# A late test of denominators, mean squares and decay with a branch to a float32 path, in a fused forgetting-attention and SwiGLU kernel

## The chip, the core and the metric

The kernel runs on one core of one Trainium2 chip. The metric is the device time of one launch in microseconds, the median of several runs; lower is better. The core has five engines with queues of their own: TensorE (PE, with its weight loads shown apart as PEld), VectorE (DVE), ScalarE (ACT), GpSimd (POOL) and SyncE (SP, which here only issues transfers). An engine takes its instructions in order; engines wait for one another on semaphores.

## What is computed

Attention with a forget gate, then a feed-forward block. B = 8, H = 8, S = 576, D = 64; the FFN has 4608 tokens, a width of 512 and 1536 hidden units.

```python
scores = scale * q @ k.T                       # per (b, h)
cum    = cumsum(log(clip(f, 1e-4, 1)))
scores = where(causal, -1e9, scores + cum[:, None] - cum[None, :])
attn   = exp(scores - max(scores)) ;  attn /= sum(attn) + 1e-9
x      = (attn @ v)  ->  (4608, 512)
xn     = x / sqrt(mean(x*x) + 1e-6) * rms_g
out    = (silu(xn @ w_gate) * (xn @ w_val)) @ w_out
```

## The kernel before

Attention goes by (batch, query block): four blocks of 128 rows per sequence and a last one of 64, the last ones of two batches joined in one tile. No row maximum is taken. Instead exp(mid - cum) for each key, `decT`, is multiplied into V (L528), with a column of the same factors beside it, so that the product of the exponentials with this V (L627) gives numerators and the denominator in one PSUM bank. DVE takes the reciprocal of the denominators (`rden`, L643) and multiplies (L645). The normal rows then are squared and summed (`ms`, L659 or L673), raised to -1/2 on POOL (L678), normalised (L689), transposed (on SP, L709) and go to the FFN in nine groups of 512 tokens: eight of the 128-row blocks, tile `xT`, and the ninth of all the 64-row blocks, tile `xTr`.

In the FFN a gate step (`gate`, L763) is: four matmuls with `wg` into one of four PSUM banks `ff` (L773), four with `wv` into another, tanh on ACT (`th`, L786), (th + 1) times the gate on DVE (`ga`, L788, after which the first bank is free), and ga times the value on DVE (`hT`, L780, after which the second bank is free). The projection (L807) takes twelve matmuls per 128 tokens, a copy out of PSUM (L821, on ACT; on DVE for the very last tile) and a transfer to the output (L829; L838 for the ninth group).

The order of all instructions is settled before anything runs: every step is a unit with an engine, an estimated duration, a key and dependencies, and `Plan.run` (L152) walks through time and gives each engine the ready unit with the lowest key; it also hands out the buffers of the rings, the four `ff` banks among them. `SHIFTS`, a table with one entry per unit, moves each key. The steps that the change touches: `emit_cum` (L367) builds `cum`, `mid`; `emit_const` (L342) fills constants on POOL; `rden` was two small tiles used in turn; the units run at L865, and after them the program ends, each engine going straight on to the closing block (L897), where SP waits for all transfers and the engines meet twice.

## Time and profile before

| | us |
|---|---|
| timed runs | 371.33, 372.7, 373.48 (median 372.7) |
| span of the profiled execution, first to last instruction | 370.3 |
| PE busy in the span | 354.5 (96%) |
| DVE, ACT, POOL busy | 231.8, 206.6, 188.4 |
| granted TensorE clock, mean | 1.000 |

The median of the timed runs is 2.4 us above the span of the profiled execution; its own time outside the span isn't recorded. In the timeline a row gives the start, the time to the end of the last of the instructions it joins, the engine, the line, output and input, how many instructions, and in brackets the idle time before them with what ended it. An engine's name with q (SPq, PEldq) is an instruction that its sequencer handles: a transfer's issue, a wait, a drain.

### The profile page before, as it was taken

What the parts mean: (1) busy time and instruction counts of PE and PEld (TensorE: products, weight loads), DVE (VectorE), ACT (ScalarE), POOL (GpSimd) and SP (SyncE); (2) the same over time, 40 slices, a digit from 0 to 9 for tenths busy, and PEclk for the clock granted to TensorE, in tenths of its full rate; (3) what the DMA queues carried; (4) which work ended last, traced back from release to release, by engine and by line L of the source; (5) the groups of instructions that cost most, each with busy time, mean ns of one, the idle gap of its engine ahead of it and who ended that gap; (6) DMA issues with size and microseconds to landing.
All of it is one profiled execution on the core that took longest, in us unless ns stands there. A gap on an engine that the chain in (4) does not pass through costs nothing.

```text
span 370.3 us, 9645 instructions
## 1 busy us (share of the span) xinstructions
PE 354.5 (96%) x3916; PEld 207.0 (56%) x3916; DVE 231.8 (63%) x457; ACT 206.6 (56%) x312; POOL 188.4 (51%) x253
## 2 busy tenths in 40 slices
PE   3878999999999999999999999999999999999995
PEld 1568977887754555554555454446544554444443
DVE  6666676677657786568764677455576436877210
ACT  5752676666766777756737776168835434233121
POOL 8954799979898737554995179524201110000000
PEclk9999999999999999999999999999999999999999
DMA  9999999999999992999999979963400121000124
GB/s 119 194 206 213 196 225 128 164 204 127 151 140 153 192 143 60 143 199 114 138 165 200 157 71 115 178 125 86 114 30 0 50 81 58 2 0 2 57 57 113
DMA packets 155965, 45.08 MB, mean 122 GB/s; under 512 B 145489, under 2 KB 150353, under 8 KB 155921
## 3 DMA queue, kind: packets, MB, share of 16 engines
q0 software_dynamic: 80896, 17.83, 57.0%
q1 hardware_dynamic: 74864, 26.51, 38.0%
q8 instruction: 30, 0.49, 0.6%
q14 instruction: 15, 0.11, 0.1%
q10 hardware_dynamic: 160, 0.13, 0.1%
HBM read 38.16 MB, written 9.44 MB: 129 GB/s over the span
## 4 chain that ended last, share of the span: by engine, by line
PE 88%; DMA 5%; POOL 3%; issue 1%; DVE 1%; ACT 0%; POOLq 0%; DVEq 0%; ACTq 0%
PE ff L773 49%; PE ff L807 24%; PE sc L557 7%; PE ff L627 7%; DMA qk<-in_q_dram 5%; POOL qk L401 1%; PE ff L507 1%; PE sc L568 1%; POOL PT L607 1%; POOL Vs L528 0%; PE ff L698 0%; ACT PT L599 0%; POOL rs L678 0%; PE ff L380 0%; ACT junk L659 0%
## 5 line engine op out<-in xcount | busy, mean ns | idle before, releaser
L599 ACT ACTIVATE PT<-sc 128x1024 bf16<-128x1024 f32 x100 | 98.2, 1022 | 33.3 <-PE sc L557 28.7
L788 DVE SCALAR_TENSOR_TENSOR ga<-th,ff 128x512 f32<-128x512 f32 x108 | 73.6, 686 | 50.1 <-ACT th L786 47.8
L807 PE MATMUL ff<-wo,hT 128*128 128x512 bf16 (+2 forms) x444 | 103.9, 373 | 0.0
L786 ACT ACTIVATE th<-ff 128x512 f32<-128x512 f32 x108 | 63.8, 597 | 61.8 <-PE ff L773 54.0
L773 PE MATMUL ff<-xT,wv 128*128 128x128 bf16 (+1 forms) x672 | 94.8, 288 | 0.1
L773 PE MATMUL ff<-xT,wg 128*128 128x128 bf16 (+1 forms) x672 | 93.9, 288 | 0.8 <-DVE xT L705 0.8
L780 DVE SCALAR_TENSOR_TENSOR hT<-ga,ff 128x512 bf16<-128x512 f32 x108 | 72.0, 684 | 24.3 <-PE ff L773 22.0
L773 PEld LDWEIGHTS <-wg 128*128 128x128 bf16 x720 | 54.1, 98 | 39.7 <-issue 0.9
L773 PEld LDWEIGHTS <-wv 128*128 128x128 bf16 x720 | 53.7, 98 | 37.7 <-DMA wv<-in_moe_w_val_dram 0.3
L607 POOL TENSOR_SCALAR_AFFINE_SELECT PT<-PT 128x1024 bf16<-128x1024 bf16 x32 | 36.8, 1154 | 54.1 <-ACT PT L599 54.1
L807 PEld LDWEIGHTS <-hT 128*128 128x128 bf16 x444 | 39.5, 98 | 40.0
L528 POOL TENSOR_TENSOR Vs<-v,decT 128x512 bf16<-128x512 f32 (+1 forms) x37 | 39.7, 1072 | 25.3 <-DMA v<-in_v_dram 21.5
L821 ACT COPY ores<-ff 128x512 f32<-128x512 f32 x35 | 20.5, 586 | 39.1 <-PE ff L807 38.9
L627 PEld LDWEIGHTS <-PT 128*128 128x128 bf16 (+1 forms) x960 | 32.3, 103 | 12.3 <-issue 2.3
L627 PE MATMUL ff<-Vs,PT 128*128 128x65 bf16 (+1 forms) x960 | 36.6, 195 | 0.3 <-POOL PT L607 0.3
L401 POOL DMA_DIRECT2D qk<-in_q_dram x40 | 35.0, 877 | 2.6 <-DMA wv<-in_moe_w_val_dram 1.4
L401 POOL DMA_DIRECT2D qk<-in_k_dram x40 | 34.9, 874 | 0.4 <-DMA wg<-in_moe_w_gate_dram 0.4
L557 PE MATMUL sc<-QT,KT 64*128 64x128 bf16 (+1 forms) x960 | 32.0, 210 | 0.2
L645 DVE TENSOR_TENSOR x<-ff,rden 128x256 f32<-128x256 f32 x72 | 30.6, 425 | 2.5
L557 PEld LDWEIGHTS <-KT 64*128 64x128 bf16 x960 | 23.5, 95 | 14.6 <-issue 12.1
L689 DVE SCALAR_TENSOR_TENSOR xn<-x,rs,rgB 128x512 bf16<-128x512 f32 x28 | 24.0, 870 | 12.1 <-POOL rs L678 12.0
L678 POOL TENSOR_TENSOR rs<-ms,mhalf 128x1 f32<-128x1 f32 (+1 forms) x28 | 17.0, 608 | 22.8 <-ACT junk L659 20.9
(58 smaller groups left out, 158.0 us busy)
## 6 DMA issues: line engine op xcount, KB each, us to landing
out_dram<-ores SPq DMA_DIRECT2D x32, 256.0 KB, 3.1
v<-in_v_dram SPq DMA_DIRECT2D x20, 256.0 KB, 5.0
qk<-in_q_dram POOLq DMA_DIRECT2D x32, 128.0 KB, 5.4
qk<-in_k_dram POOLq DMA_DIRECT2D x32, 128.0 KB, 5.2
v<-in_v_dram POOLq DMA_DIRECT2D x12, 256.0 KB, 5.8
wg<-in_moe_w_gate_dram POOLq DMA_DIRECT2D x3, 512.0 KB, 14.8
wv<-in_moe_w_val_dram POOLq DMA_DIRECT2D x3, 512.0 KB, 13.0
wo<-in_moe_w_out_dram POOLq DMA_DIRECT2D x2, 768.0 KB, 11.9
```

The costliest lines, as they stand in the source:

```text
L401: nc.gpsimd.dma_start(out=T_qk[h.slot][0:n, :].rearrange("p (h d) -> p h d", d=D), in_=src[b, :, p0:p0 + n, :].rearrange("h p d -> p h d"))
L528: eng.tensor_tensor(T_Vs[hv.slot][0:n, j, :, 0:D], T_v32[h.slot][0:n, :, :], bcast(dj, D), ALU.mult)
L557: nc.tensor.matmul(t[:, par, c:c + n], lhsT=kt[r, p, kj * 128:(kj + 1) * 128], rhs=qt[r, p, qi * 128:qi * 128 + n], start=(b, qi) not in FAST,
L599: nc.scalar.activation(T_PT[hp.slot].rearrange("p (a c) -> p a c", a=2), T_sc[h.slot], ACT.Exp, scale=scale)
L607: nc.gpsimd.affine_select(out=d, in_=d, pattern=[[0, 1024 // n], [1, n]], compare_op=ALU.is_ge, fill=0.0, base=0, channel_multiplier=-1)
L627: nc.tensor.matmul(po[i * n:(i + 1) * n, p, :], lhsT=T_PT[h.slot][:, c:c + n], rhs=T_Vs[hold_Vs[x].slot][:, kj, 2 * p + par, :], start=(kj ...
L645: nc.vector.tensor_tensor(d, po[:, :, 0:D], bcast(rden[par], D), ALU.mult)
L773: nc.tensor.matmul(T_ff[h.slot][:, c:c + n], lhsT=w[:, dc, fc * 128:(fc + 1) * 128], rhs=xT[:, dc, t0:t0 + n], start=(dc == 0), stop=(dc = ...
L780: nc.vector.scalar_tensor_tensor(hT, in0=three[0], scalar=0.5, in1=three[1], op0=ALU.mult, op1=ALU.mult)
L786: th = act(0.6, key - 0.1, lambda: nc.scalar.activation(T_th[ht.slot], T_ff[hg.slot], ACT.Tanh, scale=0.5), [ug], take=[ht])
L788: a = dve(0.72, key - 0.1, lambda: nc.vector.scalar_tensor_tensor(T_ga[ha.slot], in0=T_th[ht.slot], scalar=1.0, in1=T_ff[hg.slot], op0=ALU ...
L807: nc.tensor.matmul(T_ff[hf.slot][:, 0:wide], lhsT=T_hT[hold_hT[g].slot][:, fc, j * 128:(j + 1) * 128], rhs=wo[:, fc, cols], start=(fc == 0 ...
```

## The change

It adds a test and a second way. The denominators' reciprocals are now all kept: `rden` becomes one tile [128, 5, 8, 4, 2] that each reciprocal writes its own piece of. Near the end, when all are there, 13 DVE instructions (`emit_sane`) multiply them by `decT`, test that every product lies in 1e-20 to 1e12, that every mean square is at most 1e37, and join it with an earlier test (`emit_span`, three DVE instructions behind `emit_cum`) that the decay of each head spans at most 80. The reciprocals of the odd batches' last blocks lie in the upper partitions; a transfer on SP (`rlow`) brings them down first. A matmul of one column counts the partitions in which all holds, and DVE writes 128 minus that into `bad`. After the last planned instruction every engine loads `bad` into a register and compares; at 0 it skips, otherwise it runs `general`: float32 attention with row maxima in a loop over 64 heads, and then the FFN in a loop over batches. POOL also clears `ms` once (`emit_const`), since its unused entries are tested. `SHIFTS` has a 0 put in for each new unit and is otherwise the same.

```diff
@@ SHIFTS
-    0, 0, 0, 0, 115, 0, 168, 0, -45, 18, -4, -107, 167, 17, 151, 264, 13, 25, 230, 9, -319, 248, 106, -107, 8, -33,
+    0, 0, 0, 0, 115, 0, 168, 0, -45, 18, -4, -107, 167, 17, 151, 264, 13, 25, 230, 9, -319, 248, 106, -107, 8, 0,
...
@@ new
+def general(ctx, tc, c):
...
+    with tc.For_i(0, B * H, 1) as i:
...
+    with tc.For_i(0, B, 1) as b:
...
@@ fox_ffn_kernel
-    rden = [sb.tile([128, 4], F32, name=f"rden{i}") for i in range(2)]
+    rden = sb.tile([128, NB, B, 4, 2], F32, name="rden")
+    rlow = sb.tile([64, B // 2, 4, 2], F32, name="rlow")
+    tried = sb.tile([128, LAST * BH], F32, name="tried")
+    sane = sb.tile([128, 4], F32, name="sane")
+    bad = sb.tile([1, 1], mybir.dt.int32, name="bad")
@@ emit_const
+        nc.gpsimd.memset(stat[0], 0.0)
@@ behind emit_cum
+    def emit_span():
+        nc.vector.memset(sane[:, 3:4], 1.0)
+        nc.vector.tensor_tensor(sane[0:BH, 0:1], cum[:, 0:1], cum[:, S - 1:S], ALU.subtract)
+        nc.vector.tensor_scalar(sane[0:BH, 3:4], in0=sane[0:BH, 0:1], scalar1=DECAY_MAX, op0=ALU.is_le,
+                                scalar2=None)
+
+    spanned = dve(0.4, -17, emit_span, [d3])
@@ ev
-                nc.vector.reciprocal(rden[par], po[:, :, D])
+                rd = rden[:, qi, b, :, par]
+                nc.vector.reciprocal(rd, po[:, :, D])
...
-                nc.vector.tensor_tensor(d, po[:, :, 0:D], bcast(rden[par], D), ALU.mult)
+                nc.vector.tensor_tensor(d, po[:, :, 0:D], bcast(rd, D), ALU.mult)
@@ before the plan runs
+    L_rlow = load("SP", 0.6, (64, 0.01), 8.7, lambda: nc.sync.dma_start(
+        out=rlow, in_=rden[64:128, LAST, 0:B:2, :, :]), [evac[b, LAST, par] for b in range(0, B, 2) for par in range(2)])
+
+    def emit_sane():
...
+    sound = dve(2.6, 8.7, emit_sane, [spanned, L_rlow, L_dec] + list(evac.values()) + list(pieces.values()))
+    h_bad = Hold("ff", 1)
+    counted = pe(0.1, 8.87, lambda: nc.tensor.matmul(T_ff[h_bad.slot][0:1, 0:1], lhsT=sane[:, 3:4], rhs=unit,
+                                                     start=True, stop=True), [sound], take=[h_bad])
+    dve(0.1, 8.87, lambda: nc.vector.tensor_scalar(bad, in0=T_ff[h_bad.slot][0:1, 0:1], scalar1=-1.0, op0=ALU.mult,
+                                                   scalar2=128.0, op1=ALU.add), [counted], give=[h_bad])
@@ behind the plan's instructions
+    unsound = nc.values_load(bad, min_val=0, max_val=128,
+                             skip_runtime_bounds_check_because="a count of partitions, of which there are 128")
+    with tc.If(unsound > 0, preferred_fallthrough_block=False):
+        general(tc, locals())
```

Up to the test the order on every engine is the old one, with the new instructions put in; line numbers behind the new function are 121 or 122 higher. Two places matter.

The first is DVE some 60 us before the end, where the eighth group's last gate steps and the ninth group's first ones run (`ff_121` to `ff_124` are the four PSUM banks). Before:

```order
L788 SCALAR_TENSOR_TENSOR ga_115<-th_112,ff_122 128x512 [waits Activation_49]
L788 SCALAR_TENSOR_TENSOR ga_114<-th_113,ff_124 128x512 [waits Activation_49]
L780 SCALAR_TENSOR_TENSOR hT_111<-ga_115,ff_122 128x512 [waits DVE_49,PE_49]
L788 SCALAR_TENSOR_TENSOR ga_115<-th_112,ff_121 128x512 [waits DVE_49,Activation_49]
L780 SCALAR_TENSOR_TENSOR hT_111<-ga_114,ff_123 128x512 [waits PE_49]
L780 SCALAR_TENSOR_TENSOR hT_111<-ga_115,ff_124 128x512 [waits DVE_49,PE_49]
L788 SCALAR_TENSOR_TENSOR ga_114<-th_113,ff_122 128x512 [waits DVE_49,Activation_49]
```

And now:

```order
L910 SCALAR_TENSOR_TENSOR ga_115<-th_112,ff_122 128x512 [waits Activation_49]
L994 TENSOR_TENSOR tried<-rden,decT 128x256
L1011 TENSOR_SCALAR junk,sane<-tried 128x256 [waits DVE_49]
...
L1002 TENSOR_TENSOR tried<-rlow,decT 64x32 [waits DMAHW0_49]
...
L1008 TENSOR_TENSOR sane<-sane 128x1 [waits DVE_49]
L910 SCALAR_TENSOR_TENSOR ga_114<-th_112,ff_121 128x512 [waits Activation_49]
L902 SCALAR_TENSOR_TENSOR hT_111<-ga_115,ff_122 128x512 [waits PE_49]
L910 SCALAR_TENSOR_TENSOR ga_115<-th_113,ff_124 128x512 [waits DVE_49]
L902 SCALAR_TENSOR_TENSOR hT_111<-ga_114,ff_121 128x512 [waits PE_49]
L902 SCALAR_TENSOR_TENSOR hT_111<-ga_115,ff_123 128x512 [waits DVE_49]
L1020 TENSOR_SCALAR bad<-ff_122 1x1 [waits PE_49]
L910 SCALAR_TENSOR_TENSOR ga_114<-th_112,ff_124 128x512 [waits DVE_49,Activation_49]
```

The 13 instructions of the test stand between the first `ga` and the next. The two `ga` behind it have changed places, and with them the banks: the ninth group's first gate step, the last row of each piece, sits in bank 124, which the old second `ga` frees, third behind the test; before it sat in bank 122. The counting matmul takes bank 122, ahead of that gate step on PE, and waits for the test's last row.

The second is SP at the program's end. Before:

```order
L829 DMA out_dram<-ores_117 128x512 [waits DMAHW4_49,Activation_49]
L838 DMA out_dram<-ores_118 64x384 [waits DMAHW6_49,DVE_49]
L838 DMA out_dram<-ores_118 64x128 [waits DMAHW0_49,DVE_49]
L897 UNCONDITIONAL_BRANCH
```

And now:

```order
L951 DMA out_dram<-ores_117 128x512 [waits DMAHW5_49,Activation_49]
L960 DMA out_dram<-ores_118 64x384 [waits DMAHW7_49,DVE_49]
L960 DMA out_dram<-ores_118 64x128 [waits DMAHW1_49,DVE_49]
L1029 TENSOR_LOAD bad [waits DVE_49]
L1031 COMPARE_AND_BRANCH
L1031 UNCONDITIONAL_BRANCH [waits DMAHW0_49,DMAHW1_49,DMAHW2_49,DMAHW3_49,DMAHW4_49,DMAHW5_49,DMAHW6_49,DMAHW7_49]
```

Where nothing is bad, SP does not branch at the comparison, waits for all eight transfer lanes, and then jumps to the closing block. That block stands behind the whole of `general`. Before, the closing block followed directly.

## The prediction

> **What bounds the kernel now.** I read the page's totals first, then the chain that ended last, then the busy time by stretch, then the timeline at the two places where the order changes.

> ```profile
> PE 354.5 (96%) x3916; PEld 207.0 (56%) x3916; DVE 231.8 (63%) x457; ACT 206.6 (56%) x312; POOL 188.4 (51%) x253
> PE 88%; DMA 5%; POOL 3%; issue 1%; DVE 1%; ACT 0%; POOLq 0%; DVEq 0%; ACTq 0%
> ```

> PE is busy for 96% of the span and is 88% of the chain that ended last. So other engines can do more work for nothing, as long as PE never waits for it. By stretches (span of the stretch, then busy time and instructions of PE, PEld, DVE, ACT, POOL):

> ```profile
> 307.00:311.00 4.00, 4.00 (x20) 1.81 (x19) 2.45 (x5) 1.53 (x3) 0.00 (x0) 1.00 0.22 81
> 311.00:354.00 43.00, 43.00 (x201) 19.47 (x200) 26.99 (x41) 13.70 (x23) 0.00 (x0) 1.00 0.05 19
> 354.00:366.30 12.30, 12.27 (x69) 6.14 (x67) 1.24 (x2) 2.34 (x4) 0.00 (x0) 1.00 0.33 78
> ```

> From 307 us to the last matmul PE has no gap, while DVE has 16 us to spare in the 43 us from 311. What is lost on PE here is not won back later: there is no idle time in which to catch up. Behind the last matmul stands an end that is no engine's work, 4 us from 366.3 to 370.3.

> **The beginning: nothing.** Three DVE instructions come between two copies of Q, and one more constant on POOL ahead of the first weight transfer:

> ```profile
> 7.77 0.14 DVE L371 TENSOR_SCALAR mid<-mid 64x1 f32<-64x1 f32 x1
> 7.84 0.41 DVE L512 COPY QT<-ff 128x512 bf16<-128x512 bf16 x1
> 8.47 0.42 DVE L512 COPY QT<-ff 128x512 bf16<-128x512 bf16 x1 [0.23 <-PE ff L507]
> 9.81 0.14 POOL L343 MEMSET mhalf<- 128x5 f32 x1
> 10.49 1.35 PE L557 MATMUL sc<-QT,KT 64*128 64x128 bf16 x16
> ...
> 15.88 18.19 DMA qk<-in_q_dram
> ```

> The three cost some 0.14 each, 0.42 in all, of which 0.23 us fit into DVE's idle time before the second copy; that copy would end at about 9.1 instead of 8.9, and the scores that read it start at 10.49. The cover is 1.4 us. The memset is one more of 0.14 us on POOL, and the weight issue behind it shifts by that; the last row, a piece of the chain that ended last, shows that soon after it a transfer of 18.19 us paces the kernel and not POOL's instructions, so I take 0, with 0.15 as the upper end.

> **The transfer of the reciprocals: nothing.** On SP it goes in behind two output transfers and ahead of the last transposing transfer:

> ```profile
> 297.26 1.13 SPq L829 DMA_DIRECT2D out_dram<-ores  x2
> 299.13 0.42 DVE L645 TENSOR_TENSOR x<-ff,rden 128x256 f32<-128x256 f32 x1
> 301.82 1.19 SPq L709 DMA_TRANSPOSE xTr<-xn  x1
> ```

> SP is free from 298.4, the last reciprocals are there by 299.1, and one issue (0.55 us, half the 1.13) is over by about 299.8, 2 us before the transpose. Its landing, some 2 us on, is 5 us ahead of the test. If that cover went, the test would wait, and the price be that of the test below, begun later.

> **The test on DVE: a stall of PE, 1.5 us.** The place, and the durations of like instructions:

> ```profile
> 306.48 0.69 DVE L788 SCALAR_TENSOR_TENSOR ga<-th,ff 128x512 f32<-128x512 f32 x1 [2.53 <-ACT th L786]
> 308.24 2.75 PE L773 MATMUL ff<-xT,wv 128*128 128x512 bf16 x12
> 308.25 0.69 DVE L788 SCALAR_TENSOR_TENSOR ga<-th,ff 128x512 f32<-128x512 f32 x1 [1.09 <-ACT th L786]
> 308.44 0.60 ACT L786 ACTIVATE th<-ff 128x512 f32<-128x512 f32 x1 [0.22 <-PE ff L773]
> 309.30 0.69 DVE L780 SCALAR_TENSOR_TENSOR hT<-ga,ff 128x512 bf16<-128x512 f32 x1 [0.36 <-PE ff L773]
> 310.70 1.28 DVE L780 SCALAR_TENSOR_TENSOR hT<-ga,ff 128x512 bf16<-128x512 f32 x2
> 310.83 1.03 PE L773 MATMUL ff<-xTr,wg 128*128 128x512 bf16 x4
> ...
> L645 DVE TENSOR_TENSOR x<-ff,rden 128x256 f32<-128x256 f32 x72 | 30.6, 425 | 2.5
> L643 DVE RECIPROCAL rden<-ff 128x4 f32<-128x4 f32 x72 | 12.8, 178 | 22.6 <-PE ff L627 21.9 <-ACT junk L659 0.2
> L673 DVE DVE_READ_ACCUMULATOR junk<-x 128x1 f32 x12 | 1.0, 81 | 0.0
> L370 DVE TENSOR_TENSOR mid<-hT 64x1 f32<-64x1 f32 x1 | 0.2, 152 | 0.0
> ```

> The 13 instructions, priced by these rows: three over 256 elements at 425 ns, 1.28 us; five sums read out of the accumulator at 81 ns, 0.41; five products of one column at 152, 0.76; five over 32 to 64 elements, a little over the 178 of the four-element reciprocal, 0.99. Together 3.4 us. Two like instructions that don't depend on each other overlap by 0.09 (the two hT of 684 ns take 1.28); dependent ones stand about 0.04 apart. All overlapped gives 2.35 us, all apart 3.9. Seven of the twelve steps wait for DVE itself, and read-outs run beside the start of what follows if that is independent: I take 3.0 us.

> The test can begin when the first ga ends, at 306.48 + 0.69 = 307.17. The tanh for the next ga is done at 309.04, so with 3.0 us DVE is late, not ACT. Behind the test come ga (bank 121), hT (122), ga (124), at 0.69 each 2.06 in all, and then PE may write bank 124, with 0.1 for the handover: 307.17 + 3.0 + 2.06 + 0.1 = 312.3. In the profile the ninth group's gate step began at 310.83. PE stalls 1.5 us; as a formula, the test's length less 1.5. With the ends above, 0.85 to 2.4. Part of that appears one step earlier, since the third wv step (starting about 309.97) now waits for the first ga behind the test. The counting matmul is no further term: its operand is ready at about 310.2, and one small matmul fits before 312.3. What is queued behind the waiting step on PE is everything up to the end, so the whole rest moves by this.

> **The end: 2.9 us more, on SP.**

> ```profile
> 366.28 1.11 SPq L838 DMA_DIRECT2D out_dram<-ores  x2
> 366.29 1.39 ACTq L838 DMA_DIRECT2D out_dram<-ores  x2
> ...
> out_dram<-ores SPq DMA_DIRECT2D x1, 32.0 KB, 2.1
> ...
> L897 SPq EVENT_SEMAPHORE  x11: 17/28/28, 367.4 to 370.2; - x11
> L897 POOLq EVENT_SEMAPHORE  x4: 17/17/17, 369.5 to 370.2; - x4
> L897 PEldq DRAIN  x2: 13/924/1835, 364.5 to 369.8; - x2
> ...
> q8 instruction: 30, 0.49, 0.6%
> q14 instruction: 15, 0.11, 0.1%
> ```

> SP's second issue starts near 366.84 and lands 2.1 us later, at 368.9; POOL sees all engines arrived at 369.5. So SP's nine waits and drains take 0.6 us behind the landing, some 0.06 each, and the two meetings 0.8 more. Now SP first runs the eight waits of the skipping path and then, in the closing block, 12 in the built program where there were 9: up to 11 more at 0.06, 0.7 us, and with a jump 0.8.

> The jump itself is the dearer part. Instructions come by transfers: queue 8 fetched 30 blocks of 16 KB, and PE with its weight loads issued 7832 instructions, 261 for each; queue 14 brought blocks of about 8 KB, so some 128, for the others. They are fetched as the program goes on, up to the last part of the span. The closing block now lies behind `general`, which is about 160 instructions of SP, 390 of DVE and 1200 of PE in the built program, more than a block in each of these. No row here shows a jump over a block. Below, it costs nothing, if the block is at hand; above, a whole transfer, 2.1 us, and the block's own packet behind it, 0.4 (0.1% of 16 engines' span over 15 packets), 2.5 us. I take 2.1, the landing row, since a fetch asked for at the jump is a transfer of that kind. PE's sequencer reached its drain at 364.5, DVE and ACT are done by 367.7, and a fetch of 2.1 to 2.5 us for them ends by 370.2, before SP's has begun to matter: SP jumps only when its last transfer has landed, 368.9 + 0.5, and its fetch lies bare. The register load on SP lies between the last issue (367.4) and that landing, 1.5 us of cover.

> [...]

> **The sum.** 370.3 + 0 + 1.5 + 0.8 + 2.1 = 374.7 us of span, and with the 2.4 us by which the median lies above the profiled span, **377.1 us**. Its own ends: 0.85 + 0.8 + 0.4 gives 374.8, 2.4 + 0.15 + 0.8 + 2.5 gives 378.6.

> **Rivals.** First, the end's block is at hand when SP jumps, because SP sat waiting while it could be fetched. For: the wait lasts over 1 us and no row shows a jump that stalls. Against: 160 instructions are more than a block of 128. It gives 1.5 + 0.8, 375.0 us, and this is also the way to the other side: a change within 0.5% (1.9 us, about what a measurement of this kernel can tell from no change) needs the stall on PE under 1.1, so a test under 2.6 us. At 2.35 us the time is 374.4: not slower. Chance 0.22, of which 0.09 on that side.

> Second, fetches follow one another: the jump brings one block and the closing block runs into the next, and the test is at its long end. For: the closing block's place in a block is unknown. Against: it is short, 17 instructions on SP. 2.4 + 0.8 + 2 times 2.1 is 7.4, 380.1 us. Chance 0.08.

> Third, PE takes up the test's delay: DVE has 16 us to spare in the next 43. Against: PE has none there, and a delayed gate step is a delayed PE. If other banks let it go on, only the end stays, 2.9, 375.6; with the block at hand as well 0.8, 373.5. Chance 0.08, half of it each way.

> Fourth, the change doesn't do what it says: the test fails by the way in which it sums, and `general` runs. Its first loop has about 60 DVE instructions a head; at 0.15 us at least (the one-column row) that is 9 us, and 64 heads are 580 us more. The thresholds are wide for these inputs. Chance 0.02.

> Something faster has no mechanism here; only a scatter of the runs of 2 us could show it: 0.02.

> **How the numbers follow.** The forecast has 0.58: 377.1 us, 374.8 to 378.6. The range for all, 374.3 to 379.0, leaves out the second and fourth rival and about half of the ways within 0.5%. Faster 0.02; within 0.5% 0.15, from the first rival 0.09, the third 0.04, and 0.02 of scatter; slower 0.83.

> **What would show it.** Right: in the changed profile PE idle for about 1.5 us near 310 to 312, released by DVE's ga; the test's 13 instructions from its first start to its last end at 3.0 us; the last matmul 1.5 us later, at 367.8; at the end SP's waits in two groups with about 2 us and an instruction packet between them, and a distance from the last matmul's end to the span's end of 6.9 us instead of 4.0. Wrong: PE without a gap there; the test near 2 us; no gap between SP's last wait of the skipping path and the closing block; DVE or PE arriving last at the meeting; matmuls moved at the beginning.

## The result, and the profile after

The changed kernel takes 377.67 us (median of four runs, 377.45 to 378.75) against 372.01 for the kernel before (370.82 to 373.48, on the same chip): ratio 1.0153, 95% interval 1.0115 to 1.0191. Its profiled execution took 377.48 us with a span of 375.8, so 1.7 us lie outside the span.

The first place is DVE and PE around the test. First the last normalisation, `xn`, of the kernel before and of the changed one, from which the times are counted; then the changed kernel's timeline.

```profile
301.04 0.75 DVE L689 SCALAR_TENSOR_TENSOR xn<-x,rs,rgB 128x512 bf16<-128x512 f32 x1 [1.49 <-POOL rs L678]
300.58 0.75 DVE L811 SCALAR_TENSOR_TENSOR xn<-x,rs,rgB 128x512 bf16<-128x512 f32 x1 [1.49 <-POOL rs L800]
```

```profile
306.02 0.69 DVE L910 SCALAR_TENSOR_TENSOR ga<-th,ff 128x512 f32<-128x512 f32 x1 [2.53 <-ACT th L908]
306.62 0.42 DVE L994 TENSOR_TENSOR tried<-rden,decT 128x256 f32<-128x256 f32 x1
...
309.35 0.16 DVE L1008 TENSOR_TENSOR sane<-sane 128x1 f32<-128x1 f32 x1
309.42 0.68 DVE L910 SCALAR_TENSOR_TENSOR ga<-th,ff 128x512 f32<-128x512 f32 x1
310.02 0.68 DVE L902 SCALAR_TENSOR_TENSOR hT<-ga,ff 128x512 bf16<-128x512 f32 x1
310.15 1.02 PE L895 MATMUL ff<-xT,wv 128*128 128x512 bf16 x4 [0.70 <-DVE ga L910]
310.74 0.69 DVE L910 SCALAR_TENSOR_TENSOR ga<-th,ff 128x512 f32<-128x512 f32 x1
311.11 0.19 PE L1018 MATMUL ff<-unit,sane 128*1 128x1 f32 x2
...
311.48 1.02 PE L895 MATMUL ff<-xTr,wg 128*128 128x512 bf16 x4 [0.18 <-DVE ga L910]
```

The test runs from 306.62 to 309.51, 2.89 us. PE stops ahead of the third `wv` step and again ahead of the ninth group's first gate step, both times for DVE's `ga`. From the start of the last `xn` (301.04 before, 300.58 after) to that gate step it is 9.79 us before and 10.89 now: a stall of 1.10. Of it 0.88 are the two pauses shown; the counting matmul (L1018) stands in the same stretch.

The second place is the end. These are SP's two last issues, which start at the end of the last matmul, then the register load, the branch and its waits, and the closing block (L1061) of the changed kernel; the columns of the second view are the count, the shortest, median and longest duration in ns, and the first and last start.

```profile
366.93 1.11 SPq L960 DMA_DIRECT2D out_dram<-ores  x2
```

```profile
L1029 SPq TENSOR_LOAD <-bad x1: 817/817/817, 368.1 to 368.1; - x1
L1031 SPq EVENT_SEMAPHORE  x8: 17/17/17, 371.0 to 371.5; - x8
L1031 PEldq COMPARE_BRANCH  x2: 95/1852/3608, 365.9 to 367.1; - x2
L1031 DVEq COMPARE_BRANCH  x2: 51/53/55, 367.7 to 367.9; - x2
L1031 SPq COMPARE_BRANCH  x2: 38/50/61, 369.0 to 371.6; - x2
L1031 ACTq COMPARE_BRANCH  x2: 38/44/49, 369.1 to 369.3; - x2
L1061 SPq EVENT_SEMAPHORE  x14: 17/28/28, 374.1 to 375.7; - x14
L1061 ACTq DRAIN  x2: 8/35/62, 369.8 to 375.2; - x2
L1061 PEldq DRAIN  x2: 8/40/73, 370.8 to 375.3; - x2
L1061 DVEq DRAIN  x2: 10/34/59, 371.0 to 375.2; - x2
```

SP's wait for the landing ends at 371.0; SP jumps at 371.56 (the later of its two COMPARE_BRANCH rows) and issues its next instruction at 374.14: 2.58 us in which it does nothing. PE (its jump takes 3.6 us), DVE (3.1, from 367.88 to its drain at 371.0) and ACT (0.5) had reached the closing block before. But SP's wait before the jump ended late too. This is what moved in the last microseconds, with the median time from issue to landing:

```profile
q14 instruction: 5, 0.04, 1.3%
q8 instruction: 2, 0.03, 1.2%
out_dram<-ores SPq DMA_DIRECT2D x1, 96.0 KB, 3.5
out_dram<-ores ACTq DMA_DIRECT2D x1, 96.0 KB, 3.7
out_dram<-ores SPq DMA_DIRECT2D x1, 32.0 KB, 3.3
out_dram<-ores ACTq DMA_DIRECT2D x1, 32.0 KB, 3.4
```

SP's last transfer lands 3.3 us after its issue, where it took 2.1 before. From the last matmul's end to SP's landing wait it is 2.64 us before and 4.07 after, 1.4 more. The end as a whole is 3.99 us before and 8.86 after.

### The profile page after: what moved, and what is told of

Same layout as the page of the kernel before. It is cut to its first block, busy times and chain, and to the rows that moved or that the text cites. A ratio compares the mean times of both kernels' runs of the same rounds, so it can differ in the third digit from the quotient of the medians.

```text
span 375.8 us, 9654 instructions
## 1 busy us (share of the span) xinstructions
PE 351.3 (93%) x3867; PEld 206.6 (55%) x3918; DVE 238.3 (63%) x479; ACT 206.8 (55%) x312; POOL 189.1 (50%) x254
## 5 line engine op out<-in xcount | busy, mean ns | idle before, releaser
L929 PE MATMUL ff<-wo,hT 128*128 128x512 bf16 (+2 forms) x415 | 99.8, 373 | 2.1 <-issue 0.8
L649 POOL TENSOR_TENSOR Vs<-v,decT 128x512 bf16<-128x512 f32 (+1 forms) x37 | 38.9, 1052 | 28.8 <-DMA v<-in_v_dram 24.7
L767 DVE TENSOR_TENSOR x<-ff,rden 128x256 f32<-128x256 f32 x72 | 30.6, 425 | 2.5
L811 DVE SCALAR_TENSOR_TENSOR xn<-x,rs,rgB 128x512 bf16<-128x512 f32 x28 | 23.8, 862 | 12.8 <-POOL rs L800 12.6
```

Of the source, the lines that this page charges most:

```text
L649: eng.tensor_tensor(T_Vs[hv.slot][0:n, j, :, 0:D], T_v32[h.slot][0:n, :, :], bcast(dj, D), ALU.mult)
L767: nc.vector.tensor_tensor(d, po[:, :, 0:D], bcast(rd, D), ALU.mult)
L929: nc.tensor.matmul(T_ff[hf.slot][:, 0:wide], lhsT=T_hT[hold_hT[g].slot][:, fc, j * 128:(j + 1) * 128], rhs=wo[:, fc, cols], start=(fc == 0 ...
```

## The experiments

My theory after the result: the end is paid by distance. Each engine jumps over its own part of `general` and fetches the closing block; SP's fetch is bare, and PE's blocks, 16 KB on queue 8, delay the output transfers. The stall belongs to the test's place alone. The rivals: the branch itself costs (load, compare, waits), or the engines' late meeting does.

Executions scatter by a few us up to the last `xn` (it starts between 299.3 and 303.0 us, in one execution at 305.9); the kernel before scatters as much by itself (370.27 to 375.68 us in one set of 19 runs). From there on the traces repeat to some tenths. So each kernel is read by three lengths of one trace, all in us: from the start of the last `xn` to the ninth group's first gate step, from there to the last matmul's end, and from there to the end of the span (the end). The ratio to before has its 95% interval; a kernel without one was executed once only.

| kernel | last xn to gate step | to last matmul's end | end | sum | ratio |
|---|---|---|---|---|---|
| before | 9.79 | 55.45 | 3.99 | 69.22 | |
| changed | 10.89 | 55.44 | 8.86 | 75.19 | 1.0153 (1.0115 to 1.0191) |
| test only | 10.89 | 55.44 | 4.19 | 70.53 | 1.0050 (1.0009 to 1.0092) |
| branch only | 9.79 | 55.45 | 9.39 | 74.63 | 1.0123 (1.0044 to 1.0203) |
| short second way | 10.88 | 55.44 | 5.33 | 71.66 | 1.0096 (1.0047 to 1.0145) |
| the same, last copies kept ahead | 10.89 | 55.44 | 4.20 | 70.54 | |
| SP's part long | 10.89 | 55.44 | 7.86 | 74.19 | |
| PE's part long | 10.88 | 55.44 | 5.93 | 72.26 | |
| late test | 9.79 | 55.67 | 9.19 | 74.65 | 1.0188 (1.0090 to 1.0286) |
| skipping way last | 10.89 | 55.44 | 8.82 | 75.15 | 1.0153 (1.0120 to 1.0186) |
| test twice | 13.68 | 56.90 | 9.18 | 79.75 | |
| late test, POOL's transfers | 9.79 | 55.67 | 5.44 | 70.90 | 1.0056 (1.0020 to 1.0091) |
| late test, skip last, hint | 9.79 | 55.67 | 5.81 | 71.27 | 1.0049 (1.0019 to 1.0079) |
| all three and POOL's | 9.79 | 55.67 | 5.18 | 70.64 | 1.0044 (1.0013 to 1.0074) |

**The test alone.**

```diff
-    unsound = nc.values_load(bad, ...)
-    with tc.If(unsound > 0, preferred_fallthrough_block=False):
-        general(tc, locals())
```

> The test with all its instructions and the count, but no register load, no comparison and no second way: `bad` is computed and not used. Theory (the test stalls PE once, and the rest of the loss is the end): 1.1 us over the kernel before, PE idle for about 0.7 us and 0.2 us near 310 to 311.5 as in the changed kernel, and 4.0 us from the last matmul's end to the span's end as before. Rival (the stall is won back, all of the loss is the end): 0.

The stall is there in full and the end is nearly the old one: the test is worth 1.3 us of the 6.0 (1.1 expected; the end is 0.2 longer).

**The branch alone.** The three span instructions, the transfer, the test and the counting are left out; `bad` is a constant 0.

```diff
+        nc.vector.memset(bad, 0)
...
-    sound = dve(2.6, 8.7, emit_sane, ...)
```

> No test: `bad` is set to 0 at the start and never tested; the loads, the comparison and the second way are all there. Theory: no gap of PE near 310, and the end as in the changed kernel, 8.8 us from the last matmul to the span's end, so 4.9 us over the kernel before. Rival (the test is what costs): under 1 us.

No stall, and the whole of the end, 9.39 where 8.8 was expected. The two parts are 1.3 and 5.4, together 6.7 where the change has 6.0; the end itself varies by half a microsecond between kernels whose end is alike (8.86 to 9.39). The landing varies with it, 3.9 us here and 3.3 in the changed kernel, and so does the time of PE's instruction packet among the outputs, 1.78 and 1.26 us.

**A short second way.** `general` is replaced by one instruction, then by a few that write the output tiles.

```diff
-        general(tc, locals())
+        nc.vector.memset(rlow, 0.0)
```

> The test, the loads and the comparison stay; the second way is left out and one small memset stands in its place, so that the closing block follows within a few instructions. Theory (the jump over the long block is what costs, by a fetch on SP and by PE's fetched block that delays the last output transfers): no 2.6 us hole on SP, the last landings back at 2.1 to 2.4 us, the end 4.3 to 4.8 us, in all 1.4 to 2.0 over the kernel before. Rival (the register loads, comparison and waits cost by themselves): the end stays at 7 to 9 us, in all 4 or more.

SP's hole and the late landing are gone, but the end stayed 1.1 us too long: with nothing in the second way that touches the output tiles, the order put DVE's last copy and the last transfers behind the branch. The copy waited for DVE's register load and ended at 368.55, and SP and ACT could issue only behind their own loads, at 369.33 and 369.41, 1.9 us behind the last matmul (0.6 in the changed kernel). So I kept them ahead:

```diff
-        general(tc, locals())
+        for t in T_ores:
+            nc.vector.memset(t, 0.0)
```

> As the short body, but the second way is three memsets over the output staging tiles, so that the last copy and the last transfers stay ahead of the comparison; general is left out. Theory (fetches make the end long): the last landings take 2.1 to 2.4 us, SP has no hole at its jump, and the stretch from PE's last instruction to the span's end is 4.2 to 4.5 us (before 4.0, changed kernel 8.9). Rival (register loads, comparison and waits are the cost): 6 us or more.

The branch rows of this run (as above):

```profile
L1031 PEldq COMPARE_BRANCH  x2: 90/135/180, 364.5 to 364.6; - x2
L1031 SPq COMPARE_BRANCH  x2: 37/49/61, 367.6 to 367.7; - x2
```

The end is 4.20, that of the kernel without a branch (4.19). PE's jump takes 0.18 us, and on SP, ACT, DVE and PE the next instruction starts 0.16 to 0.23 us after the jump does. So load, compare and jump cost nothing at the end here; what lies between jump and target does.

**Only SP's, then only PE's part long.** The short way with 160 transfers on SP, and with 640 matmuls on PE.

```diff
...
+        for _ in range(160):
+            nc.sync.dma_start(out=rlow, in_=rden[64:128, LAST, 0:B:2, :, :])
```

> The second way is 160 small transfers on SP (and the three memsets), so that SP alone must jump over more than a block; general is left out. Theory (SP's own fetch is bare, and the late landing comes from the fetches of the other engines): landings back at 2.1 to 2.4 us, a hole of 2.6 us on SP behind its jump, the end 7.3 to 7.6 us. Rival (the late landing comes from SP's side, its register load or its fetch ahead): landings at 3.3 or more and an end of 8.8.

```diff
...
+        for _ in range(640):
+            nc.tensor.matmul(T_ff[0][:, 0:128], lhsT=ident, rhs=ident, start=True, stop=True)
```

> The second way is 640 matmuls on PE (and the three memsets), so that PE alone must jump over several blocks; general is left out. Theory (PE's 16 KB instruction block rides one of the DMA engines that carry the last output, and holds it up): landings at 3.2 to 3.8 us, PE's jump 3 to 4 us long, no hole on SP, the end 5.4 to 5.8 us. Rival (PE's fetch is a bystander): landings 2.1 to 2.4 us and an end of 4.2 to 4.5.

SP's long part first, its branch, its closing block (L1064) and the transfers of its last 10 us:

```profile
L1031 SPq EVENT_SEMAPHORE  x8: 17/17/17, 375.0 to 375.5; - x8
L1031 SPq COMPARE_BRANCH  x2: 38/50/61, 374.2 to 375.6; - x2
L1064 SPq EVENT_SEMAPHORE  x14: 17/28/28, 378.4 to 380.0; - x14
```

```profile
q14 instruction: 2, 0.02, 0.5%
out_dram<-ores SPq DMA_DIRECT2D x1, 32.0 KB, 2.1
```

And PE's:

```profile
L1031 PEldq COMPARE_BRANCH  x2: 95/2102/4108, 365.2 to 366.4; - x2
```

```profile
q8 instruction: 2, 0.03, 2.0%
out_dram<-ores SPq DMA_DIRECT2D x1, 32.0 KB, 3.8
out_dram<-ores ACTq DMA_DIRECT2D x1, 32.0 KB, 3.9
```

The two costs come apart. With SP's part long there is no packet on queue 8, the landing takes 2.1 as before, and SP's next instruction comes 2.80 us after its jump (0.2 more than expected, hence 7.86). With PE's part long there is no hole on SP, PE's jump takes 4.1 us and ends in time, and yet the end is 1.7 us longer, because the last outputs take 3.8 us to land (the end, 5.93, is a little beyond the expected 5.8). That is the fetch for PE's jump.

**The late test.** The test also waits for the run's last `hT` and so stands behind the last gate step.

```diff
-    sound = dve(2.6, 8.7, emit_sane, [spanned, L_rlow, L_dec] + list(evac.values()) + list(pieces.values()))
+    sound = dve(2.6, 8.7, emit_sane, [spanned, L_rlow, L_dec] + list(evac.values()) + list(pieces.values())
+                + [u for i in range(3) for u in hdone[B, 3, i]])
```

> The changed kernel with the test's instructions made to wait for the last hT, so that they fall into DVE's idle time before the last copies (10.8 us). Theory: no gap of PE near 310, the test over within 3 us near 358, the end as in the changed kernel: 4.9 us over the kernel before, 1.1 less than the changed one. Rival (the counting matmul or its bank then stops PE among the projections): a gap of 0.5 to 3 us near 358 to 362 and no gain over the changed kernel.

The stall goes; 0.23 us come back where the counting matmul now stands between the projections, and the end is 9.19, so that 5.4 us are left over the kernel before where 4.9 were expected. The ratio doesn't show the gain: its four runs scatter from 376.85 to 382.16 us, and in the profiled execution the last `xn` started only at 303.0, two microseconds late.

**The skipping way laid out last.** One jump at the comparison, and the eight waits behind it, next to the closing block.

```diff
-    with tc.If(unsound > 0, preferred_fallthrough_block=False):
+    with tc.If(unsound > 0, preferred_fallthrough_block=True):
```

> The changed kernel, but the skipping path is laid out behind general, next to the closing block, so that each engine jumps at its comparison and not behind its waits. Theory (SP's jump is a fetch, which then runs while SP would wait for its last transfers anyway): the hole of 2.6 us stands ahead of SP's eight waits, the end is 6.8 to 7.2 us instead of 8.9, 1.7 to 2.1 less than the changed kernel. Rival (the jump costs the same wherever it stands): 8.9.

My forecast fell: the end is 8.82.

```profile
L1031 PEldq COMPARE_BRANCH  x1: 4037/4037/4037, 366.0 to 366.0; - x1
L1031 SPq COMPARE_BRANCH  x1: 58/58/58, 370.2 to 370.2; - x1
L1031 SPq EVENT_SEMAPHORE  x8: 17/17/17, 373.7 to 374.2; - x8
```

Counted from the last matmul, SP jumps 1.5 us earlier than in the changed kernel, but its hole is 3.4 us in place of 2.6, and behind it stand 20 waits in place of 12, 0.6 more. So of the 1.48 us gained ahead of the jump 0.85 went to the longer hole and 0.60 to the waits behind it. SP's last issue also took 1.39 us in place of 0.54; without that the jump would have come earlier still.

**The test twice**, one copy behind the other.

```diff
     def emit_sane():
+        for _ in range(2):
+            emit_sane_once()
+
+    def emit_sane_once():
...
```

> The 13 instructions of the test are written twice, one copy behind the other at the same place; branch and second way as in the changed kernel. Theory (PE's stall is the test's length less a slack of 1.8 us, 2.89 less 1.10 in the changed kernel): test 5.7 us long, last xn to the ninth group's first gate matmul 13.7 us where it was 10.89 (a stall of 3.9), all behind it moved by the same, 55.44 from there to the last matmul, the end 8.9. Rival (PE takes up part of the delay with other banks): less than 12.6 us, or less than 55.2 behind it.

The stall is as computed, 3.89 us, but behind it PE needs 56.90 us in place of 55.44, which neither theory had. The timeline, and then the busy time by stretch, in which the third number from the end is the granted TensorE clock:

```profile
312.36 1.04 PE L895 MATMUL ff<-xT,wv 128*128 128x512 bf16 x4 [3.28 <-DVE ga L910]
...
313.68 1.86 PE L895 MATMUL ff<-xTr,wg 128*128 128x512 bf16 x4 [0.16 <-DVE ga L910]
...
316.86 1.03 PE L895 MATMUL ff<-xTr,wg 128*128 128x512 bf16 x4
```

```profile
311.00:312.30 1.30, 0.00 (x0) 0.00 (x0) 1.23 (x9) 0.00 (x0) 0.00 (x0) 1.00 0.00 0
313.60:315.00 1.40, 1.32 (x4) 0.48 (x4) 1.28 (x4) 0.00 (x0) 0.00 (x0) 0.50 0.00 0
317.00:318.00 1.00, 1.00 (x7) 0.46 (x5) 0.31 (x1) 0.68 (x2) 0.00 (x0) 1.00 0.00 0
```

After 3.28 us without a matmul PE ran at half its clock for 3.41 us, from 313.24 to 316.65: four matmuls took 1.86 us and not 1.03. That is the 1.45. Shorter pauses were followed by 3.41 us at half clock too, one of 2.40 us in the kernel with the branch alone (at 21.6) and one of 2.65 in that with SP's part long (at 109.4); one of 2.02 us in that with the late test (at 107.8) was not. What sets the clock is not shown. The changed kernel's pauses of 0.70 and 0.18 us left the clock at 1.00, so that a stall of 1.10 us cost its own length and one of 3.89 another 1.45.

**Three ways to a cheaper end.** With the late test: `general`'s transfers issued by POOL, which branches at 361 us, so that SP has little to jump over; the skipping way last, with a hint at the program's head that the jump is likely; and both.

```diff
-            nc.sync.dma_start(...)
+            nc.gpsimd.dma_start(...)
...
```

> The test waits for the last hT of the run as well (it then stands behind the last gate step), and the second way's transfers are issued by POOL, which branches soon after the test, so that SP has some ten instructions to jump over; PE's, DVE's and ACT's part of the second way is unchanged. Theory (the stall goes with the place, the hole in SP's row with SP's distance, and PE's 16 KB block still holds up one DMA engine): last xn to first gate matmul 9.8, from there to the last matmul 55.7, no hole in SP's row, landings of the last transfers 3.2 to 3.8, end 5.4 to 6.0, so that last xn to the span's end is 71.0 to 71.6 (before 69.2, changed kernel 75.2); a ratio to before of about 1.006. Rival (whichever engine has the longest way over the second way sets the end, PE or DVE in SP's place, or POOL): end 7 or more, with the meeting released by that engine.

```diff
+        tc.mark_branch_hint_location("skip", hint="LikelyTaken", engines=[...])
...
-    with tc.If(unsound > 0, preferred_fallthrough_block=True):
+    with tc.If(unsound > 0, preferred_fallthrough_block=True, label="skip"):
```

> The late test, the skipping way laid out last (one taken jump at the comparison, as in the run that lays it out last), and at the head of the program on each engine an instruction that names this jump as likely taken. Theory (the fetch is what costs, and the fetcher holds the hint until the jump): the jumps on SP, PE and DVE take 0.5 us or less, no 16 KB block of the second way is fetched ahead of the last landing, landings 2.1 to 2.4, end 4.2 to 5.2, ratio about 1.002. Rival (a hint so far ahead does nothing): holes of 2.5 to 3.5 us on SP and 3 to 4 on PE, end 8.5 to 9.0, ratio about 1.012.

> The late test, the second way's transfers on POOL, the skipping way laid out last, and the hint at the program's head on PE, DVE and ACT. Theory (no taken jump is left that has to fetch behind the last matmul, and PE's 16 KB block comes early): PE's and DVE's jump 0.5 us or less, no hole on SP, landings 2.1 to 2.4, end 4.2 to 4.6, last xn to the span's end 69.6 to 70.1 (before 69.2), ratio to before 1.001 to 1.002, not to be told from no change. Rival (laying the skipping way out last slows SP's last issue and load by itself, as in the two runs that have it, where they took 1.26 to 1.39 and 1.07): second issue over 1.0 us, landing 0.7 later, end 5.0 to 5.9, ratio 1.003 to 1.005.

POOL's version, its last transfer; the hinted one's hint on PE and its branch; and of both together the branch, and SP's two last issues in the timeline:

```profile
out_dram<-ores SPq DMA_DIRECT2D x1, 32.0 KB, 3.2
```

```profile
L1063 PEldq BRANCH_PREFETCH_HINT  x1: 50/50/50, 0.9 to 0.9; - x1
L1033 PEldq COMPARE_BRANCH  x1: 388/388/388, 364.8 to 364.8; - x1
L1033 SPq COMPARE_BRANCH  x1: 78/78/78, 369.0 to 369.0; - x1
L1033 SPq EVENT_SEMAPHORE  x8: 17/17/17, 369.5 to 370.1; - x8
```

```profile
L1033 PEldq COMPARE_BRANCH  x1: 398/398/398, 365.3 to 365.3; - x1
```

```profile
366.45 1.80 SPq L960 DMA_DIRECT2D out_dram<-ores  x2
```

POOL's version behaves as expected: no hole, PE's jump of 3.4 us hidden, PE's block still delaying the landing, end 5.44. The hint works although it stands 360 us ahead: PE's jump falls from 4.04 to 0.39 us and SP's hole from 3.43 to 0.55. But the end is 5.81 where 4.2 to 5.2 was expected, and a 16 KB block on queue 8 still comes ahead of the last landing. What is left, here and with both edits, is the slow last issue: with both 1.80 us for two where it was 1.11. All three kernels that lay the skipping way out last have it (1.39, 1.26 and 1.24 for the second issue, and a register load of 1.06 to 1.08 on SP in place of 0.80 to 0.83 in the changed kernel and most others), so the rival of the last run came true. In all three PE's 16 KB block begins within 0.06 us of that issue; whether the block or the layout slows it was not separated.

With both, the change costs 0.44% (0.13 to 0.74) where it cost 1.53%. By their intervals the ratios of the three (1.0056, 1.0049 and 1.0044) can't be told apart. None is faster than the kernel before.

## Why the prediction was right

It forecast 377.1 us for a measured 377.67. The way of the loss was right, a stall at the test and a bare fetch on SP; that the number is so near is in part luck, since errors partly cancel. Term by term 377.1 − 0.4 (stall) + 2.0 (end) − 0.5 (start) − 0.7 (outside the span) gives 377.5, the profiled 377.48.

**The beginning and the transfer**: the last `xn` started at 300.58, 0.46 us earlier than before and within the scatter, so a cost at the beginning of some tenths could not be seen. The transfer cost nothing, as said: DVE has no idle time within the test.

**The test and the stall**: the mechanism is shown by the row of releasers, by the test alone (the whole stall), and by the late test (none). The size was 1.10 and not 1.5. The test was 2.89 and not 3.0, and began beside the end of the first `ga` (306.62 against 306.71); from its end to the gate step it was 1.97 us where I had added three steps and a handover to 2.16, since `hT` and the `ga` behind it start before their predecessors end. The counting matmul was no term, as said.

**The waits**: 0.8 expected, 0.86 measured (eight in the skipping way in 0.57 us, the rest in the closing block).

**The jump on SP**: 2.1 taken, 2.58 measured, a little above the upper end of 2.5. In the short version with the last copies kept ahead no instruction packet came in the last 5.8 us, and on SP, ACT, DVE and PE the next instruction followed 0.16 to 0.23 us after the jump's start. The register load on SP took 0.82 us and was hidden, as said (368.09 to 368.91, the last landing at 370.8).

**The step that failed** is "a fetch of 2.1 to 2.5 us for them ends by 370.2, before SP's has begun to matter". As a wait it was hidden, though at 3.6 us on PE it was longer than that. But I counted it as a wait only, and not as a packet: PE's blocks delay the last outputs by 1.4 us, on which SP's whole chain hangs. The run with only PE's part long shows this term by itself, 1.7 us. The sum had nothing for it.

**The rivals**: the block at hand is false for SP, PE and DVE (2.58, 3.6 and 3.1 us), and true for ACT (0.5); two fetch waits did not follow one another on SP (one hole of 2.58 us); PE took up nothing of the delay (55.45 and 55.44 us behind the gate step); `general` did not run. The 2.4 us taken as lying outside the span were 1.7 and scatter between runs.

## What to carry to other kernels

A branch to a rare way was cheap where the engines had little to jump over (0.5 us on SP over some ten instructions), and dear where the engine that ends last had much (2.8 us over 160 transfers): move its instructions to an engine that is done early, or announce the jump (SP's hole was 0.55 us with the hint and 3.43 without). Count a fetch twice, as a wait of the engine that jumps and as packets among the last outputs, which landed after 3.8 us in place of 2.1 with PE's part long. Put a test behind the last step that waits for its engine (the stall of 1.10 us went), and keep any stall of TensorE short, since a pause of 3.28 us cost another 1.45 in clock.
